# Half-slab loads, statistics in three pieces and later folds in the head of a spectral and feed-forward kernel

## The chip, the cores and the metric

The kernel runs on one core of one Trainium2 chip. The metric is the device time of one execution in microseconds (us). A run also gives the mean clock granted to TensorE. Medians are of all executions of a run; ratios, with their 95% intervals, use executions of the fast state only. "PE" is TensorE, "PEld" its weight load, "DVE" VectorE, "ACT" ScalarE, "POOL" GpSimd, "SP" SyncE.

## The reference, cut to what matters

```python
x = A_x                                # 1 x 2048 x 640, bf16
xn = _layernorm(x, axis=-1)
X = rfft2(xn); X = X * (w_r + 1j*w_i)  # w_r, w_i: 2048 x 321
s = irfft2(X)                          # spectral branch
g = _silu((_gelu(xn @ w_gate) * (xn @ w_up)) @ w_down)   # feed-forward branch, 640 -> 1536 -> 640
# ... the output is x + s * g
```

Both branches need the layer norm of x. TensorE does the feed-forward products and the Fourier transforms, which are products with tables.

## The kernel before

x is held as 16 slabs of 128 rows by 640. Each task of the kernel (a load, a pass, a group of products) is given to a planner written in the kernel itself, with a cost, a rank and what it must follow. The planner simulates the engines and fixes in which order each engine gets its instructions, and on which engine a copy runs. So a changed cost or dependency can change the order of instructions anywhere in the program.

```python
# loads of the first slabs
nc.scalar.dma_start(out=X[:, 1, :], in_=xv[:, 1, :])
nc.scalar.dma_start(out=X[:, 3, :], in_=xv[:, 3, :])
# ...
load_x(0, 1)                       # slab 0, whole, SyncE
x_in[1] = x_in[0]
load_x(2, 3)

# statistics of a slab on VectorE: one task
def moments(e):
    for g in range(2):
        nc.vector.bn_stats(out=STAT[:, n1, 6*g:6*g+6], in_=x[:, 320*g:320*g+320])
    nc.vector.bn_aggr(out=MVA[:, n1, :], in_=...)
    nc.vector.tensor_scalar_add(out=var, in0=var, scalar1=1e-5)
t = add(moments, "DVE", (1200, 1340), (2, n1), after=after, use=[sX])
# then root: (var)^-0.5 on GpSimd; apply: normalise on VectorE; turn_pe: transpose on TensorE and copy out
# ...
        if n1 % 2:                 # two slabs normalised: fold them for the spectral branch
            fold(n1 // 2, [aps[n1 - 1], aps[n1]])
```

`fold` is four adds and subtracts on VectorE, two pairs of products on TensorE ("fold products"), two copies and a store. Two more parts come up in the experiments. The spectral weights are gathered row by row, 32 times, by GpSimd:

```python
for pm in range(2):
    for ri, wsrc in enumerate((A_w_r, A_w_i)):
        nc.gpsimd.indirect_dma_start(out=sw.tile[:, pm, ri, 0:L], out_offset=None, in_=wsrc,
            in_offset=bass.IndirectOffsetOnAxis(ap=LANE[:, 2*G+pm:2*G+pm+1], axis=0))
```

and four tables (TI, I1T, IM, IT) are loaded from ScalarE's queue near 65 us.

## Time and profile before

| | before |
|---|---|
| three runs, first set | 218.63, 215.86, 215.78 us |
| the run that was profiled | 205.17 us, span 203.0, clock 1.0 |
| PE busy | 196.6 us, 97% of the span |

And in the list of transfers, the gathers have a time to landing, 3.0 us:

```profile
WF<-in_A_w_r_dram,LANE POOLq DMA_INDIRECT x16, 3.0
```

### The profile page before, as it was taken

What the parts mean: (1) busy time and instruction counts of PE and PEld (TensorE: products, weight loads), DVE (VectorE), ACT (ScalarE), POOL (GpSimd) and SP (SyncE); (2) the same over time, 40 slices, a digit from 0 to 9 for tenths busy, and PEclk for the clock granted to TensorE, in tenths of its full rate; (3) what the DMA queues carried; (4) which work ended last, traced back from release to release, by engine and by line L of the source; (5) the groups of instructions that cost most, each with busy time, mean ns of one, the idle gap of its engine ahead of it and who ended that gap; (6) DMA issues with size and microseconds to landing.
All of it is one profiled execution on the core that took longest, in us unless ns stands there. A gap on an engine that the chain in (4) does not pass through costs nothing.

```text
span 203.0 us, 3956 instructions
## 1 busy us (share of the span) xinstructions
PE 196.6 (97%) x1481; PEld 115.7 (57%) x1481; DVE 160.7 (79%) x340; ACT 108.4 (53%) x185; POOL 57.4 (28%) x83
## 2 busy tenths in 40 slices
PE   7899999999999999999999999999999999999991
PEld 2584444576545555577765544457764555556781
DVE  2899989998235289999999999932489799997764
ACT  2686963344524567788786633323454565454421
POOL 3514532065027505476478200000002022221100
PEclk9999999999999999999999999999999999999999
DMA  6999999799499601143143501119402244333422
GB/s 184 313 318 338 355 338 253 120 296 177 151 300 277 220 3 28 37 120 112 37 127 115 181 0 66 66 66 336 184 0 59 74 129 118 85 99 116 126 76 65
DMA packets 30947, 30.78 MB, mean 152 GB/s; under 512 B 10545, under 2 KB 27457, under 8 KB 30929
## 3 DMA queue, kind: packets, MB, share of 16 engines
q1 hardware_dynamic: 27696, 24.16, 39.7%
q0 software_dynamic: 2368, 5.30, 10.5%
q10 hardware_dynamic: 864, 1.09, 1.7%
q8 instruction: 11, 0.18, 0.4%
q14 instruction: 8, 0.06, 0.1%
HBM read 20.70 MB, written 7.86 MB: 141 GB/s over the span
## 4 chain that ended last, share of the span: by engine, by line
PE 78%; DMA 9%; DVE 5%; SPq 4%; ACT 1%; issue 1%; ACTq 0%; DVEq 0%
PE pg L808 19%; PE pu L808 19%; PE pu L868 12%; PE pg L868 12%; DMA X<-in_A_x_dram 5%; SPq L296 4%; DMA D<-mc 3%; PE sp L621 3%; PE sp L754 3%; PE sp L696 2%; PE sp L730 2%; PE sp L591 2%; DVE uT L824 1%; PE sp L614 1%; PE sp L748 1%
## 5 line engine op out<-in xcount | busy, mean ns | idle before, releaser
L808 PE MATMUL pg<-xnT,Wg 128*128 128x512 bf16 (+1 forms) x270 | 60.7, 355 | 0.0
L808 PE MATMUL pu<-xnT,Wu 128*128 128x512 bf16 (+1 forms) x270 | 60.7, 355 | 0.0
L820 ACT ACTIVATE ge<-pg 128x512 bf16<-128x512 f32 x48 | 28.6, 596 | 38.9 <-PE pg L808 38.5
L868 PEld LDWEIGHTS <-uT 128*128 128x128 bf16 x396 | 37.5, 98 | 13.2
L824 DVE TENSOR_TENSOR uT<-pu,ge 128x512 bf16<-128x512 f32 x48 | 33.0, 689 | 12.6 <-PE pu L808 11.3
L808 PEld LDWEIGHTS <-Wg 128*128 128x128 bf16 x270 | 24.6, 98 | 22.7
L808 PEld LDWEIGHTS <-Wu 128*128 128x128 bf16 x270 | 24.2, 98 | 20.8
L868 PE MATMUL pg<-Wd,uT 128*128 128x320 bf16 (+2 forms) x204 | 31.8, 293 | 0.0
L868 PE MATMUL pu<-Wd,uT 128*128 128x320 bf16 (+1 forms) x192 | 31.0, 297 | 0.0
L289 ACT CAST ma<-sp 128x644 bf16<-128x644 f32 (+1 forms) x29 | 23.1, 795 | 13.3 <-PE sp L754 6.6
L833 POOL DMA_DIRECT2D xr<-in_A_x_dram x16 | 8.6, 547 | 72.8 <-DVE res L856 72.8
L547 POOL DMA_INDIRECT WF<-in_A_w_r_dram,LANE x16 | 16.7, 1047 | 18.0 <-DVE mc L661 15.0
L547 POOL DMA_INDIRECT WF<-in_A_w_i_dram,LANE x16 | 17.4, 1085 | 4.9 <-issue 4.6
L415 POOL TENSOR_TENSOR RSTD<-MVA,mh 128x1 f32<-128x1 f32 x16 | 9.5, 595 | 22.6 <-DVE MVA L399 22.1
L877 ACT ACTIVATE th<-pg 128x320 f32<-128x320 f32 (+2 forms) x17 | 7.2, 426 | 16.1 <-PE pg L868 15.6
L882 DVE SCALAR_TENSOR_TENSOR G<-th,pg 128x320 bf16<-128x320 f32 (+2 forms) x17 | 8.0, 468 | 7.9 <-ACT th L877 7.9
L882 DVE SCALAR_TENSOR_TENSOR G<-th,pu 128x320 bf16<-128x320 f32 (+1 forms) x16 | 7.7, 479 | 4.1 <-ACT th L877 4.1
L397 DVE BATCH_NORM_STATS2 STAT<-X 128x6 f32<-128x320 bf16 x18 | 7.9, 481 | 3.1 <-DMA X<-in_A_x_dram 3.1
L289 ACT CAST IU<-sp 128x640 bf16<-128x640 f32 x13 | 9.0, 691 | 2.5 <-PE sp L696 2.3
L289 ACT CAST mc<-sp 128x640 bf16<-128x640 f32 x11 | 7.2, 693 | 3.4 <-PE sp L491 3.4
L877 ACT ACTIVATE th<-pu 128x320 f32<-128x320 f32 (+1 forms) x16 | 7.0, 438 | 3.1 <-PE pu L868 2.4
L674 DVE TENSOR_TENSOR R<-Y 64x644 bf16<-64x644 bf16 x16 | 7.9, 491 | 0.4
(79 smaller groups left out, 238.0 us busy)
## 6 DMA issues: line engine op xcount, KB each, us to landing
BU<-D SPq DMA_DIRECT2D x8, 640.0 KB, 7.1
D<-mc SPq DMA_DIRECT2D x8, 320.0 KB, 4.1
D<-IU SPq DMA_DIRECT2D x8, 320.0 KB, 2.4
xr<-in_A_x_dram POOLq DMA_DIRECT2D x16, 160.0 KB, 3.0
out_dram<-res SPq DMA_DIRECT2D x15, 160.0 KB, 1.8
Wg<-in_B_w_gate_dram SPq DMA_DIRECT2D x6, 320.0 KB, 6.1
Wu<-in_B_w_up_dram SPq DMA_DIRECT2D x6, 320.0 KB, 7.1
Wd<-in_B_w_down_dram SPq DMA_DIRECT2D x2, 960.0 KB, 8.5
```

Of the source, the lines that this page charges most:

```text
L289: return nc.scalar.copy(out=out, in_=in_) if e == "ACT" else nc.vector.tensor_copy(out=out, in_=in_)
L296: return add(lambda e: nc.sync.dma_start(out=out() if callable(out) else out, in_=in_() if callable(in_) else in_), "SP", (430, 430), rank ...
L397: nc.vector.bn_stats(out=STAT[:, n1, 6 * g:6 * g + 6], in_=x[:, 320 * g:320 * g + 320])
L415: nc.gpsimd.tensor_tensor(out=rstd, in0=var, in1=mh, op=ALU.pow)
L547: nc.gpsimd.indirect_dma_start(out=sw.tile[:, pm, ri, 0:L], out_offset=None, in_=wsrc, in_offset=bass.IndirectOffsetOnAxis(ap=LANE[:, 2 * ...
L808: nc.tensor.matmul(ps.tile[:, lo:hi], lhsT=w[:, c, t * P:(t + 1) * P], rhs=xnT[:, c, grp * 512 + lo:grp * 512 + hi], start=(c == 0), stop= ...
L820: nc.scalar.activation(out=ge.tile, in_=pg.tile, func=ACT.Gelu_apprx_tanh)
L824: nc.vector.tensor_tensor(out=u.tile, in0=pu.tile, in1=ge.tile, op=ALU.mult)
L833: nc.gpsimd.dma_start(out=sx.tile, in_=xv[:, n1, :])
L868: nc.tensor.matmul(ps.tile[:, 0:hi - lo], lhsT=uT[grp, t].tile[:, j * P:(j + 1) * P], rhs=Wd[:, t, lo:hi], start=(t == 0), stop=(t == 11))
L877: nc.scalar.activation(out=th.tile[:, 0:hi - lo], in_=ps.tile[:, 0:hi - lo], func=ACT.Tanh, scale=0.5)
L882: nc.vector.scalar_tensor_tensor(out=G2.tile[:, lo:hi], in0=th.tile[:, 0:hi - lo], scalar=1.0, in1=ps.tile[:, 0:hi - lo], op0=ALU.add, op1 ...
```

## The change

The intent is an earlier first product. What runs before the first 512-wide product, some 14 us, is called the head. The halves of slabs 0 and 1 go to both queues, so that slab 0 is there first. The statistics are three tasks, so that the normalise of slab 0 can go ahead of slab 1's last piece. And the first folds wait until slab 3 is normalised.

```diff
-    nc.scalar.dma_start(out=X[:, 1, :], in_=xv[:, 1, :])
+    for n in range(2):
+        nc.scalar.dma_start(out=X[64:P, n, :], in_=xv[64:P, n, :])
@@
-    load_x(0, 1)
-    x_in[1] = x_in[0]
+    for n in range(2):
+        seq[0] += 1
+        x_in[n] = dma(X[0:64, n, :], xv[0:64, n, :], (0, -4, seq[0]), 163840, use=[sX])
     load_x(2, 3)
-    t = keep_warm(4, [t, x_in[0]], 0)
-    keep_warm(3, [t, x_in[1]], 1)
+    t = keep_warm(3, [t, x_in[0]], 0)
+    keep_warm(2, [t, x_in[1]], 1)
@@
-            t = add(moments, "DVE", (1200, 1340), (2, n1), after=after, use=[sX])
+            t = add(lambda e: half(e, 0), "DVE", (445, 445), (2, n1), after=after, use=[sX])
+            t = add(lambda e: half(e, 1), "DVE", (445, 445), (2, n1), after=[t], use=[sX])
+            t = add(moments, "DVE", (345, 450), (2, n1, -1), after=[t])
@@
-        if n1 % 2:
+        if n1 == 3:
+            for j in range(2):
+                fold(j, [aps[k] for k in range(4)])
+        elif n1 % 2 and n1 > 3:
             fold(n1 // 2, [aps[n1 - 1], aps[n1]])
# ... and planner constants: start of the DMA wire 2600 -> 1900, hold of the normalises
# 700 (slabs 0, 1) -> 250 (slabs 0 to 3), later statistics behind slab 3's copy, a few costs
```

More of the change, by code (lines that the diff above doesn't have):

```diff
@@ L25 @@
 DUMP = None
+VERB = False
 def make_tables():
@@ L135, in __init__ @@
         self.tasks, self.slots = [], {t: [] for t in bufs}
-        self.wire = 2600.0
+        self.wire = 1900.0
     def add(self, emit, eng, cost, rank, after=(), new=(), use=(), size=0, slow=1.0, hold=0):
@@ L194, in run @@
             self.free[e] = now + occ
+            if VERB: print(f"{now:9.0f} {occ:6.0f} {t.done or 0:9.0f} {e} {t.emit.__qualname__.split('kernel.<locals>.')[-1]} {t.rank}")
             t.done = now + lat
@@ L358, in go @@
                                  start=True, stop=True, skip_group_check=True)
-        return add(go, "PE", (n * 430, n * 430), (0, -9), after=after, new=[] if heat.users else [heat], use=[idle, sX] + ([heat] if heat.users else []))
+        return add(go, "PE", (n * 390, n * 390), (0, -9), after=after, new=[] if heat.users else [heat], use=[idle, sX] + ([heat] if heat.users else []))
     t = add(blank, "DVE", (330, 400), (0, -9), new=[idle])
     t = keep_warm(6, [t])
-    load_x(0, 1)
-    x_in[1] = x_in[0]
+    for n in range(2):
+        seq[0] += 1
+        x_in[n] = dma(X[0:64, n, :], xv[0:64, n, :], (0, -4, seq[0]), 163840, use=[sX])
     load_x(2, 3)
-    t = keep_warm(4, [t, x_in[0]], 0)
-    keep_warm(3, [t, x_in[1]], 1)
+    t = keep_warm(3, [t, x_in[0]], 0)
+    keep_warm(2, [t, x_in[1]], 1)
     x_in[3] = tab_in["id"] = x_in[2]
@@ L392, in stats, with half @@
         eng = engs[0]
-        after = [x_in[n1]] + ([aps[3]] if n1 > 3 else [])
+        after = [x_in[n1]] + ([turned[3]] if n1 > 3 else [])
+        def half(e, g):
+            nc.vector.bn_stats(out=STAT[:, n1, 6 * g:6 * g + 6], in_=x[:, 320 * g:320 * g + 320])
         def moments(e):
-            for g in range(2):
-                nc.vector.bn_stats(out=STAT[:, n1, 6 * g:6 * g + 6], in_=x[:, 320 * g:320 * g + 320])
             nc.vector.bn_aggr(out=MVA[:, n1, :], in_=STAT[:, n1, :].rearrange("p (g s) -> p g s", g=2))
@@ L427, in go @@
                                     op0=ALU.subtract if eng == "DVE" else ALU.add, op1=ALU.mult)
-        return add(go, "DVE", (360, 510), (1, n1, 0), hold=700 if n1 < 2 else 0, after=[root], new=[sxn] if new else [], use=[sX] if new else [sX, sxn])
+        return add(go, "DVE", (430, 530), (1, n1, 0), hold=250 if n1 < 4 else 0, after=[root], new=[sxn] if new else [], use=[sX] if new else [sX, sxn])
     def turn_pe(n1, ap):
```

## The prediction

> **What bounds the kernel now.** I read the page's busy shares first, then busy time in stretches, then the head in order of time.
>
> ```profile
> PE 196.6 (97%) x1481; PEld 115.7 (57%) x1481; DVE 160.7 (79%) x340; ACT 108.4 (53%) x185; POOL 57.4 (28%) x83
> ...
> PE   7899999999999999999999999999999999999991
> DVE  2899989998235289999999999932489799997764
> ```
>
> TensorE (PE) is busy 97% of a span of 203.0 us. A busy PE need not be an efficient one, so I checked start times: in the steady stretch five 512-wide matmuls start every 1.08 us, 0.216 us each, with nothing between groups. PE is therefore the bound by order of work. The question is only where it idles or does useless work. By stretch (columns: stretch, length, then busy us and instruction counts of PE, weight load, VectorE (DVE), ScalarE (ACT), GpSimd (POOL), then clock, DMA share, GB/s):
>
> ```profile
> 7.00:8.00 1.00, 0.45 (x5) 0.28 (x5) 0.55 (x3) 0.34 (x1) 0.83 (x3) 1.00 1.09 349
> 8.00:9.00 1.00, 0.93 (x16) 0.93 (x17) 0.97 (x4) 0.80 (x2) 0.44 (x1) 1.00 1.20 306
> 9.00:10.00 1.00, 0.98 (x19) 0.81 (x17) 0.96 (x5) 0.25 (x1) 0.68 (x1) 1.00 1.20 307
> ...
> 35.00:40.00 5.00, 4.87 (x29) 2.48 (x27) 5.00 (x12) 1.57 (x4) 0.00 (x0) 1.00 0.74 119
> ...
> 195.00:203.00 8.00, 3.96 (x41) 3.36 (x39) 4.16 (x13) 1.81 (x5) 0.00 (x0) 1.00 0.18 61
> ```
>
> From 10 us to the last matmul near 199 us PE loses about 0.13 us in all. After that come 4 us of tail (last tanh, gate, residual, store), which the change does not touch. What is left is the head: the first useful product (gate weights by slab 0) starts at 8.40 us. Before it PE runs 13 throwaway matmuls[...], and the transposes of slabs 0 and 1. The head in order of time (start, length, engine, line, operation, then idle before it and what ended it):
>
> ```profile
> 0.73 0.39 ACTq L340 DMA_DIRECT2D X<-in_A_x_dram  x1
> 0.73 0.89 SPq L296 DMA_DIRECT2D X<-in_A_x_dram  x2
> 4.22 0.89 DVE L397 BATCH_NORM_STATS2 STAT<-X 128x6 f32<-128x320 bf16 x2 [3.06 <-DMA X<-in_A_x_dram]
> 5.45 0.88 DVE L397 BATCH_NORM_STATS2 STAT<-X 128x6 f32<-128x320 bf16 x2
> 5.62 0.57 POOL L415 TENSOR_TENSOR RSTD<-MVA,mh 128x1 f32<-128x1 f32 x1 [3.06 <-DVE MVA L399]
> 6.61 0.15 DVE L399 TENSOR_SCALAR MVA<-MVA 128x1 f32<-128x1 f32 x1
> 6.68 0.44 DVE L425 TENSOR_SCALAR s<-X,MVA,RSTD 128x640 bf16<-128x640 bf16 x1
> 7.17 0.45 PE L436 MATMUL sp<-ident,s 128*128 128x128 bf16 x5 [0.27 <-DVE s L425]
> 7.66 0.69 ACT L289 COPY xnT<-sp 128x640 bf16<-128x640 bf16 x1 [0.80 <-PE sp L436]
> 8.40 0.44 PE L808 MATMUL pg<-xnT,Wg 128*128 128x128 bf16 x5
> ```
>
> The reader is to see one chain: slab 0 arrives, statistics, power of -1/2 on GpSimd, normalise, transpose, copy, first product. Two links are longer than need be. The data are visible at 4.22 us. And 1/std of slab 0 is ready at 5.62 + 0.57 = 6.19, but the normalise starts at 6.68, because slab 1's whole statistics stand before it on VectorE: 0.49 us lost.
>
> [...] slabs 0 and 1 start together at 0.73, and the DMA share is 1.05 in the 3 to 4 us stretch. So the halves do not move bytes faster; they change which bytes come first. [...] the throwaway matmuls start 0.41 to 0.43 us apart until 6.31 us, and at the transposes at 7.17 us the weight loads stand 0.056 us apart.
>
> **The change, part by part.**
>
> 1. *Halves over both queues.* In the DMA view of the first 9 us in 40 slices of 0.225 us, I summed GB/s by slice: 164 KB had been moved by about 2.8 us, 328 KB by about 3.35. Before, slabs 0 and 1 interleave, so slab 0's last byte comes near 3.35 and is seen at 4.22. After, both halves of slab 0 go first, so it needs 164 KB: about 0.5 us earlier. I take its statistics to start at 3.7. Slab 1 should be seen near 4.2 as before. Slabs 2 and 3 stand behind the same bytes; one more issue on each queue (0.43 us) is hidden as the DMA engines are full by then. Seen by ACT at 5.08 before; I allow up to 5.2.
>
> 2. *Statistics in three pieces.* No work is added: two halves of 0.44 us, then aggregate and add (0.40 us to the end). It lets the normalise of slab 0 slip between. By hand, with the durations above: slab 0 halves 3.7 to 4.6, its aggregate and add end at 5.0, POOL 5.1 to 5.7, slab 1 halves 4.95 to 5.8, normalise of slab 0 at 5.8 (before 6.68: 0.9 earlier). Slab 1's aggregate then waits for it, ends at 6.6, its power 6.65 to 7.25, its normalise at about 7.35 (before 7.56).
>
> 3. *Transpose and copy of slab 0.* Transposes at about 6.3, ready for the copy at 6.8. ACT holds slab 2's two passes, which ended at 6.86 before and will not end earlier. So copy 6.88 to 7.57, first product at about 7.65, against 8.40: 0.75 us earlier. Here ACT takes over a little of the wait.
>
> 4. *PE from there to the first 512-wide product.* Before, 8.40 to 14.38 = 5.98 us: 16 groups of 0.28 (4.48), transposes of slabs 2 and 3 (0.56), one fold product (0.54), so 0.40 of bubbles. After: 16 groups, three transposes (0.84), the fold product later instead: 5.32 us, from 7.65 to 12.97. Before without the fold: 13.84. So PE is ahead by 0.87 us, if no bubble comes.
>
> 5. *Folds after the norm of slab 3.* Eight VectorE operations of 0.40 us (3.2 us) move behind the normalises. Two of them stood between slab 2's normalise at 9.20 and slab 3's at 10.37, so slab 3 comes about 1 us earlier: by hand its normalise is at about 8.9, its columns are ready near 10.3, and PE wants them at about 11.7. The later folds do not hurt: spectral products start near 63 us, and PE has feed-forward work until then.
>
> 6. *Two throwaway matmuls fewer, new cost constants.* Off the path. The constants alter the order that the kernel's own planner chooses all through the program. I cannot price that; PE's list is the same work.
>
> Sum: 0.87 us, all in the head, passing to the end because PE is dense behind it. 215.86 - 0.87 = 214.99.
>
> **Rivals.**
>
> *A: the arrival does not move.* If the four halves interleave on the engines, or first-byte ramp dominates (GB/s climbs from 28 to 273 between 1.6 and 2.9 us), slab 0 is still seen at 4.2. Only the split helps: normalise at 6.3, gain some 0.35 us, 215.5.
>
> *B: another wait takes its place.* The up weights: about 1,360 KB precede their end, which the summed stretches put near 6.6 us, seen perhaps at 7.4, against a need at 7.9. ACT's slab 2 passes: if slab 2 arrives 0.3 later, the copy moves with it. [...] Each would leave 0.2 to 0.6 of gain: 215.3 to 215.7.
>
> *C: the moved folds or the new order open holes later.* VectorE is at 95% or more from 80 to 130 us, and PE lives there on feed-forward work put between. Against it: PE was at 10.00 of 10.00 in each of those stretches, so there is stock. If the new order is unlucky, 0.5 to 1.5 us come back and the time is 215.5 to 216.5.
>
> *D: hidden.* That an earlier head is absorbed wholly (215.9) would need PE idle time later; the stretches show nearly none.
>
> **Range and chances.** I weigh the main line at about 60%, A and B at 25%, C at 15%. Before's three times span 215.78 to 218.63, so one slow run can lift a median. Predicted 215.0 us, range 214.1 to 216.3. Faster by over 2% needs 4.3 us, more than half of all time before the first useful product: 1%. Slower by over 2% needs a broken plan or a slow median: 2%. Within 2%: 97%.
>
> **What would show it.** Slab 0's first statistics at 3.7, not 4.2; its normalise between slab 1's halves and aggregate, at 5.8; first product near 7.65; the first 512-wide product near 13.0; no PE hole over 0.3 us between 8 and 13 us; last matmul near 198. Wrong: slab 0 not earlier, the copy of slab 0 waiting on ACT past 7.0[...], or PE under 4.8 of 5 in any later stretch.

## More of the kernel before

By its time, the profile that I read for the prediction is one of the quick kind of chip (which chip it was is not on record), and the times are of the slow kind.

Beside what the prediction shows, two views of this profile will matter. First the timeline near 65 us (start, length, engine, line, operation; in brackets the idle time before it and what ended it):

```profile
64.90 1.24 PE L808 MATMUL pg<-xnT,Wg 128*128 128x512 bf16 x5
...
65.38 0.44 ACTq L321 DMA_DIRECT2D IT<-tab_it  x1
66.18 0.60 ACT L820 ACTIVATE ge<-pg 128x512 bf16<-128x512 f32 x1 [1.15 <-PE pg L808]
```

The gate product that starts at 64.90 ends at 66.14, and the gelu that reads it starts at 66.18, 0.04 us later. Then the busy times by stretch (columns: stretch, length, busy us and instruction count of PE, PEld, DVE, ACT, POOL, then clock, DMA share, GB/s):

```profile
62.00:76.00 14.00, 14.00 (x111) 7.52 (x109) 7.99 (x13) 7.54 (x10) 5.88 (x7) 1.00 0.50 153
90.00:125.00 35.00, 35.00 (x284) 21.36 (x283) 33.73 (x65) 23.76 (x37) 15.74 (x16) 1.00 0.32 95
```

TensorE has no idle time in either stretch.

## The result, and the profile after

| | before | after |
|---|---|---|
| median of 6 runs, same set | 216.41 us (215.78 to 218.63) | 213.46 us (211.47 to 214.04) |
| ratio of fast runs | | 0.9866 (0.9817 to 0.9915) |
| profiled run | span 203.0, quick kind | span 209.7, clock 0.991, slow kind |

A ratio is the mean time of one kernel's fast runs over the mean of the other's of the same rounds, so it is not quite the ratio of the medians. The change gained 2.9 us where at most 1.8 lay in the range: the direction was right, the size was not, and the gain is under 2%. The page after, and its stretches:

```profile
PE 196.4 (94%) x1463; PEld 117.1 (56%) x1479; DVE 158.5 (76%) x337; ACT 109.9 (52%) x188; POOL 55.6 (27%) x83
...
PE   7599999999999789997998999999999999999991
```

```profile
7.00:8.00 1.00, 0.45 (x5) 0.38 (x6) 0.96 (x5) 1.00 (x3) 0.58 (x2) 0.98 1.04 325
8.00:9.00 1.00, 0.56 (x6) 0.56 (x6) 0.83 (x5) 0.39 (x1) 0.92 (x3) 0.50 1.09 337
9.00:10.00 1.00, 1.00 (x13) 1.00 (x11) 0.92 (x3) 0.30 (x1) 0.33 (x1) 0.50 1.20 301
...
35.00:40.00 5.00, 4.95 (x27) 2.49 (x27) 4.50 (x12) 2.48 (x4) 0.73 (x1) 1.00 0.90 118
...
62.00:76.00 14.00, 12.07 (x84) 6.28 (x84) 5.20 (x7) 4.63 (x7) 6.71 (x8) 1.00 0.54 175
90.00:125.00 35.00, 32.52 (x278) 20.83 (x279) 31.08 (x60) 21.86 (x33) 18.84 (x19) 1.00 0.34 100
```

Three things stand out. PE's work is the same, 196.4 us busy, but the span is 6.7 us longer than in the profile before. The head is not faster: from 8 to 10 us the clock column says 0.50, and only 6 and 13 products start where 16 and 19 did before. And PE is idle for 1.93 us between 62 and 76 and for 2.48 us between 90 and 125, where it was idle for nothing before. The head in order of time:

```profile
3.73 0.89 DVE L400 BATCH_NORM_STATS2 STAT<-X 128x6 f32<-128x320 bf16 x2 [2.58 <-DMA X<-in_A_x_dram]
5.71 0.89 DVE L400 BATCH_NORM_STATS2 STAT<-X 128x6 f32<-128x320 bf16 x2 [0.66 <-DMA X<-in_A_x_dram]
6.03 0.74 ACT L407 ACTIVATE th<-X 128x640 bf16<-128x640 bf16 x1 [1.66 <-DMA X<-in_A_x_dram]
6.52 0.43 DVE L432 TENSOR_SCALAR s<-X,MVA,RSTD 128x640 bf16<-128x640 bf16 x1
7.00 0.45 PE L443 MATMUL sp<-ident,s 128*128 128x128 bf16 x5 [0.68 <-DVE s L432]
8.44 0.69 PE L818 MATMUL pg<-xnT,Wg 128*128 128x128 bf16 x5 [0.98 <-ACT xnT L291]
```

Slab 0 comes earlier, at 3.73, and slabs 1 and 2 come later, at 5.71 and 6.03; they were there by 5.45 and 5.08. The first product is at 8.44, so the head alone explains no gain at all in this execution. The stretch near 66 us and the transfers:

```profile
65.78 1.24 PE L818 MATMUL pg<-xnT,Wg 128*128 128x512 bf16 x5
...
67.60 0.44 ACTq L323 DMA_DIRECT2D IT<-tab_it  x1
70.54 0.60 ACT L830 ACTIVATE ge<-pg 128x512 bf16<-128x512 f32 x1 [3.27 <-PE sp L584]
```

```profile
WF<-in_A_w_r_dram,LANE POOLq DMA_INDIRECT x16
```

The gate product of 65.78 ends at 67.02, and its gelu starts at 70.54, 3.5 us later. ScalarE had nothing else to do but issue table loads until 68.04. And the gathers have no time to landing any more, but neither has any other transfer on this page (the loads of BU had 7.1 us before), so this tells of signals that are missing from the record and not of slower gathers. The late gelu belongs to the kind of chip and not to the change, as is shown next.

### The profile page after: what moved, and what is told of

Read it like the earlier page. It is cut to its first block, busy times and chain, and to the rows that moved or that the text cites.

```text
span 209.7 us, 3946 instructions
## 1 busy us (share of the span) xinstructions
PE 196.4 (94%) x1463; PEld 117.1 (56%) x1479; DVE 158.5 (76%) x337; ACT 109.9 (52%) x188; POOL 55.6 (27%) x83
## 4 chain that ended last, share of the span: by engine, by line
PE 88%; DVE 4%; DMA 2%; ACT 2%; issue 2%; SPq 1%; DVEq 0%
PE pu L818 24%; PE pg L818 23%; PE pg L878 12%; PE pu L878 12%; PE sp L706 3%; PE sp L631 3%; PE sp L764 3%; PE sp L740 2%; DMA X<-in_A_x_dram 2%; PE sp L601 2%; PE sp L497 2%; PE sp L624 1%; PE sp L758 1%; DVE uT L834 1%; PE sp L443 1%
## 5 line engine op out<-in xcount | busy, mean ns | idle before, releaser
L818 PE MATMUL pg<-xnT,Wg 128*128 128x512 bf16 (+1 forms) x262 | 60.0, 358 | 1.3 <-ACT xnT L291 1.0
L818 PEld LDWEIGHTS <-Wu 128*128 128x128 bf16 x270 | 24.8, 99 | 21.6 <-issue 0.4
L422 POOL TENSOR_TENSOR RSTD<-MVA,mh 128x1 f32<-128x1 f32 x16 | 10.3, 646 | 19.6 <-DVE MVA L404 19.0
L291 ACT CAST IU<-sp 128x640 bf16<-128x640 f32 x12 | 8.1, 692 | 2.5 <-PE sp L706 2.5
L291 ACT CAST Z<-sp 128x1024 bf16<-128x1024 f32 x7 | 7.0, 1017 | 4.3 <-PE sp L706 1.9
L291 ACT CAST mc<-sp 128x640 bf16<-128x640 f32 x13 | 8.4, 698 | 0.8 <-PE sp L498 0.8
```

What stands on the lines that cost most here:

```text
L291: return nc.scalar.copy(out=out, in_=in_) if e == "ACT" else nc.vector.tensor_copy(out=out, in_=in_)
L422: nc.gpsimd.tensor_tensor(out=rstd, in0=var, in1=mh, op=ALU.pow)
L818: nc.tensor.matmul(ps.tile[:, lo:hi], lhsT=w[:, c, t * P:(t + 1) * P], rhs=xnT[:, c, grp * 512 + lo:grp * 512 + hi], start=(c == 0), stop= ...
```

## The experiments

**Set 1, a slow chip (before 213.62 us, 211.51 to 215.03, 11 runs): what comes from the loads, and what from the order?** The kernel before and the changed one again, and the two halves of the change crossed. `e3` is the kernel before with half loads and no other difference, `e4` the changed kernel with whole loads; the order is the same as in the kernel each comes from.

```diff
# e3: old order, half loads
-    load_x(0, 1)                                   (and slab 1 whole from ScalarE)
+    X[0:64, 0], X[0:64, 1] from SyncE; X[64:128, 0], X[64:128, 1] from ScalarE, in the old task's place
# e4: changed order, whole loads
-    halves
+    slab 0 whole from SyncE, slab 1 whole from ScalarE, in the new tasks' places
```

> The kernel before, unchanged, for its profile on a chip where it takes its usual time: the profile shown of it (span 203.0 us, 205.17 us) is 10.7 us shorter than its timed runs (median 216.41 us). Theory H (only the head changed): the usual run has the same dense TensorE from the first product on and a later first product[...]. Theory O (order): the usual run has TensorE holes of 5 to 10 us in all between 60 and 130 us, in the spectral stage, as the profile of the changed kernel has (about 6 us there); then the profile shown of before was of a lucky execution. [...] Expected time 216 us, ratio 1.00.

> The changed kernel again, for a second profile and its ratio on this chip. The first profile has its first product at 8.44 us, half clock from 8.0 to 11.4 us and about 6 us of TensorE holes between 60 and 120 us. Theory H: ratio 0.985 to 0.99 again. Theory G: if the half-clock window comes and goes by execution, times spread by about 1.7 us. Theory O: holes at the same places as in the first profile.

> The kernel before with the loads of slabs 0 and 1 as partition halves over both queues, and nothing else: the order of instructions on TensorE, VectorE, ScalarE and GpSimd is exactly that of before. If the loads bring the gain, the ratio to before is near 0.987; if they bring only slab 0's earlier arrival (0.5 us), 0.997 to 0.998; if the late arrival of slab 1 (seen at 5.7 us in the profile of the changed kernel, against 4.2 or earlier in that of before) costs as much, 1.00 or above.

> The changed kernel with the loads of before (slab 0 whole on one queue, slab 1 whole on the other), and nothing else: the order of instructions on TensorE, VectorE, ScalarE and GpSimd is exactly that of the changed kernel. If the gain is in the order (theory O, or the pieces of the statistics and the folds), the ratio to before stays at 0.985 to 0.99, or is lower as slab 1 comes earlier; if the halves bring it, the ratio goes to 1.00.

| run | median us | ratio to before (95%) |
|---|---|---|
| e1, before again | 213.31 | 1.0014 (0.9970 to 1.0058) |
| e2, after again | 211.77 | 0.9905 (0.9859 to 0.9951) |
| e3, old order, half loads | 213.25 | 0.9988 (0.9942 to 1.0035) |
| e4, new order, whole loads | 211.37 | 0.9900 (0.9851 to 0.9948) |

Within about 0.5% the half loads bring nothing; the gain is in the order. And e1 is the first look at the kernel before on a slow chip. (Its profiled execution, 211.76 us at a clock of 0.996, is one of the faster ones; 8 of the 11 of this set have 0.983 to 0.992.)

```profile
65.50 1.24 PE L808 MATMUL pg<-xnT,Wg 128*128 128x512 bf16 x5
...
66.27 0.44 ACTq L321 DMA_DIRECT2D IT<-tab_it  x1
70.58 0.60 ACT L820 ACTIVATE ge<-pg 128x512 bf16<-128x512 f32 x1 [4.65 <-PE pu L808]
```

```profile
62.00:76.00 14.00, 11.21 (x83) 5.95 (x81) 4.67 (x6) 5.42 (x8) 6.83 (x8) 1.00 0.57 182
90.00:125.00 35.00, 32.98 (x285) 21.23 (x283) 30.98 (x61) 24.21 (x36) 18.21 (x19) 1.00 0.33 100
```

The same product and the same gelu as in the profile before, but 3.84 us between the product's end and the gelu (70.58 less 65.50 less 1.24) instead of 0.04. TensorE is idle for 2.79 us in the first stretch and 2.02 us in the second. So the late gelu is no work of the change; it belongs to the kernel before on this chip. The engines themselves are not slower there: the instructions of VectorE take 161.0 us in e1 and 160.7 in the quick profile, those of ScalarE 108.0 and 108.4.

To see where time is gained I read how far TensorE lags behind its own work: the start of a product, less the time that all columns before it take at full pace. The lag grows where PE waits, and also where it does not: by 3.4 us from 65 to 186 us of work in the quick profile, where PE is busy for 188.83 of the 189 us from 10 to 199. So the rows are read against each other. In us, at so much work done:

```
work done                      5.5     15     40     60     65    100    186
old order, quick (shown)      8.26   8.34   8.73   8.80   9.24  10.87  12.62
old order, slow  (e1)         7.72   7.80   8.48   9.40  12.70  17.50  19.26
new order, slow  (e4)         7.09   7.16   8.14   8.21  10.90  15.69  17.46
```

Of the 1.80 us between e1 and e4 at the end, 0.63 stand after the head. Part of that is lost by 40 us of work (0.34), and by 60 it is 1.19: fold products no longer wait for copies between 38 and 51 us (PE is busy for 18.19 of the 19 us from 35 to 54 in e1, for all 19.00 in e4). By 65 it is 1.80, since the hole near 73 us is shorter (idle from 62 to 76: 2.79 us in e1, 2.34 in e4), and behind that nothing is added.

**Set 2, which landed on a quick chip (before 204.87 us, 204.58 to 205.92, 11 runs): spliced orders, and the table loads moved.** For a splice the planner is bypassed: its order and engines are written out as a list, the first part from one kernel and the rest from the other. The kernel with the whole list of one kernel gives that kernel back, instruction for instruction (but for throwaway products). The loads are whole, and both splices have the 11 throwaway products of the changed kernel, not the 13 of the old one.

```diff
-        for t in plan.run():
-            t.emit(t.on)
+        for w in ORDER.split():            # e5: new order's tasks of its first 14 us, then the old order
+            t = plan.tasks[int(w[:-1])]     # e6: old order's tasks of its first 14.6 us, then the new order
+            t.on = ENG[w[-1]]
+            t.emit(t.on)
# e7 (new order, whole loads) and e8 (before): the four tables
-   nc.scalar.dma_start(out=flat(tiles[k]), in_=tabs[k])
+   nc.sync.dma_start(out=flat(tiles[k]), in_=tabs[k])
```

> Whole loads. Every instruction that the changed plan starts in its first 14 us stands in the changed order (split statistics, folds after the norm of slab 3, two throwaway products fewer); everything behind it stands in the order and on the engines of the kernel before, written out as a fixed list. Theory H (the gain is the head's, passed on whole): all of the gain of the changed order with whole loads, that is about 2 us under the kernel before (ratio 0.990). Theory M (the head gives only what the lag of TensorE showed at 5.5 us, 0.6 us, and the rest comes from the order behind it, where the products of the folds no longer wait for the copies between 38 and 51 us and the hole near 70 us is shorter): 0.4 to 0.8 us under the kernel before, ratio 0.997, with holes at 38 to 51 us still there.

> Whole loads. The first 14.6 us of the plan in the order of the kernel before (statistics in one go, first fold before slab 3's norm), everything behind it in the order and on the engines of the changed kernel, as a fixed list. Theory H: nothing, ratio 1.00. Theory M: 1.2 to 1.6 us under the kernel before, ratio 0.993, and no holes over 0.3 us at 38 to 51 us. If both this run and the one with the new head gain, and the two gains add up to about 2 us, the parts are independent.

> Changed order with whole loads, and one more thing: the four table loads that ScalarE issues near 65 us are issued by SyncE at the same place of the program. Theory T (ScalarE stands still for 2.5 to 4 us behind its own table loads, and that makes the hole near 70 us): the gelu behind them starts at once, the hole of TensorE at 72 to 73 us goes, and the time falls by 1.5 to 2.5 us against the same order with the loads on ScalarE, to a ratio of about 0.98 against the kernel before. Theory S (ScalarE waits for something else, and the loads only stand beside it): the same gap is there at the same place and the ratio stays 0.990.

> The kernel before, with the four table loads of ScalarE issued by SyncE at the same place. Theory T: the hole of about 3 us near 73 us goes, the ratio is 0.985 to 0.99. Theory S: no change, ratio 1.00. If the change gained because its order made this stall shorter, the two kernels with the loads on SyncE differ by less than the two with them on ScalarE (under 2 us).

| run | median us | ratio to before (95%) |
|---|---|---|
| e5, new head, old rest | 205.24 | 1.0002 (0.9978 to 1.0026) |
| e6, old head, new rest | 207.43 | 1.0115 (1.0088 to 1.0142) |
| e7, new order, tables on SyncE | 206.04 | 1.0064 (1.0034 to 1.0095) |
| e8, before, tables on SyncE | 204.88 | 0.9998 (0.9974 to 1.0021) |

The expectations were written for a before of 213, and none of the gains came. Here nothing of the change gains. e5's head is 0.65 us ahead after 5.5 us of work (lag 7.61 against 8.26), and it is lost at one fold product of the old order, which came too soon for VectorE:

```profile
24.83 0.39 PE L537 MATMUL sp<-mb,F1T 128*128 128x512 bf16 x1 [0.65 <-DVE mb L524]
```

e7 keeps its head's lead up to 95 us of work (lag 10.02 at 97, against 10.70 in the profile before), and then waits: by the lag 0.28 us near 103.7 and 0.91 us here, of which the view shows 0.74 as idle:

```profile
109.48 0.32 PE L624 MATMUL sp<-FT,zt 32*128 32x161 bf16 x7 [0.74 <-DVE IU L291]
```

That is a wait of the new order's own: a spectral product stands ahead of a copy that VectorE has not reached. The same hole, with 0.74 to 0.87 us idle, is in every profile with the new order behind the head, on both kinds of chip. e6 loses more than e7. In the three of its runs with a clock of 0.992, the profiled one among them, the head is one cause: the clock was at half from 8.1 to 11.5 us, and the first 512-wide product came 1.2 us later after slab 0 than in e8. The other three took 207.1 us on average, still 2.2 over the kernel before; what the seam of the splice costs was not separated.

**Set 3, a slow chip again (before 214.63 us, 211.91 to 217.40, 11 runs): is the stall ScalarE's own?**

```diff
# e12, kernel before, right behind the last table load on ScalarE
+                if k == "it":
+                    for _ in range(3):
+                        nc.scalar.copy(out=still, in_=flat(T2)[:, 0:1024])
```

> The changed kernel as it is, a third time, because the calls so far landed on two kinds of chip: the kernel before took 213.6 us in the first call of experiments and 204.9 us in the second. Theory K (what the change is worth depends on the kind of chip: on the slow kind, where ScalarE stands still behind its table loads, the new order hides part of that; on the quick kind there is nothing to hide and the new order's own waits near 104 and 109 us cost what its head saves): if this call's before is near 205 us, ratio 1.00 to 1.01, not faster; if it is near 213.5 us, ratio 0.985 to 0.992 again. Theory O (the new order is better anywhere): ratio 0.99 on either.

> The kernel before with the four table loads of ScalarE issued by SyncE, again, for the other kind of chip. If before is near 213.5 us here: theory T (the stall belongs to ScalarE's own loads) says 208 to 211 us, the 3 us hole near 73 us gone and perhaps what follows from it; theory S (ScalarE waits for something else) says 213.5. If before is near 205: 204.9 as in the call before.

> The changed order with whole loads and the tables on SyncE, again, for the other kind of chip. If before is near 213.5 us here: theory T says 208 to 209.5 us, and no longer better than the kernel before with the same edit if the change's gain was only in hiding the stall; theory S says 211.4. If before is near 205: 206.0 as in the call before.

> The kernel before with three copies of 128x1024 (about 3 us) put on ScalarE right behind its last table load, which do nothing for the result: the stall of the slow kind of chip made on purpose. On a chip where before takes 205 us: if that stall alone is what parts the two kinds, 210 to 213 us, with a hole of TensorE of about 3 us near 73 us and further holes between 90 and 115 us; if it is only one of several causes, 207 to 209 us. On a chip where before takes 213.5: 214 to 217 us if the copies add to the stall, 213.5 if they run inside it.

| run | median us | ratio to before (95%) |
|---|---|---|
| e9, after | 212.17 | 0.9931 (0.9867 to 0.9996) |
| e10, before, tables on SyncE | 213.78 | 1.0002 (0.9944 to 1.0060) |
| e11, new order, whole loads, tables on SyncE | 210.05 | 0.9842 (0.9778 to 0.9906), unclear at 2% |
| e12, before, 3 us of copies | 214.84 | 1.0054 (0.9984 to 1.0124) |

The theory that ScalarE stands still behind its own loads has fallen: without them (e10) the kernel before takes the same time, and e11's gelu still waits 3.25 us. (e11 is 2.1 us under e9, but differs from it by the whole loads as well as by the tables, so I draw nothing from that.) e12 shows the same from the other side. Three copies of 3.2 us fitted into the wait and cost little or nothing:

```profile
66.28 3.20 ACT L326 COPY still<-T 128x1024 bf16<-128x1024 bf16 x3 [0.82 <-issue]
70.13 0.60 ACT L826 ACTIVATE ge<-pg 128x512 bf16<-128x512 f32 x1 [0.64 <-PE pu L814]
```

The gelu came at 70.13 with the copies and at 70.58 without (in e1, on another slow chip). So ScalarE is waiting for something other than itself, and I read it as a signal that arrives late. I listed the recorded signals of TensorE (its semaphore counter) in that stretch, in us:

```
before, quick: 63.10 63.55 64.00 65.08 66.16 67.23 67.46 67.68 68.76 69.84 70.48 71.56
before, slow (e1): 63.70 64.15 64.89 67.72 70.56 72.01 72.06 72.12 72.19 72.26 73.94
```

On the quick chip there is one per group of products. On the slow one they come 2.8 us apart, and then several at once. Such gaps stand on slow chips at 64.9 to 72, 90 to 93, 99 to 101 and 107 to 113 us in e1, each time while packets of GpSimd's gathers run (which also run from 83 to 88 us without a gap). The trace of e1 keeps fewer signals (113 of all from 58 to 76 us, against 298), but what is missing is of the DMAs (81 against 249): of this counter of TensorE it has 224 records in all, against 227 in the quick profile. So the bursts are not gaps left by lost records. Whether the signal came late, or only its record, the list cannot tell; the late gelu is a measured start.

**Set 4, a slow chip (before 216.25 us, 213.74 to 217.56, 27 runs): the splices again, and the gathers taken away.** e15 and e16: plain loads of as many rows of the same size, on GpSimd at the same places. Their outputs are wrong, which doesn't matter for the times. e16 is the changed kernel as it is, with its half loads.

```diff
-    nc.gpsimd.indirect_dma_start(out=sw.tile[:, pm, ri, 0:L], out_offset=None, in_=wsrc,
-        in_offset=bass.IndirectOffsetOnAxis(ap=LANE[:, 2*G+pm:2*G+pm+1], axis=0))
+    nc.gpsimd.dma_start(out=sw.tile[:, pm, ri, 0:L], in_=wsrc[P*(2*G+pm):P*(2*G+pm)+P, :])
```

> The changed order for the first 14 us and the old order behind it, whole loads, again, for the slow kind of chip. Theory M (head 0.6 us, the rest of the gain from the order behind it): ratio 0.996 to 0.998. Theory H (all of it from the head): 0.990. If this call's before is near 205 us: 1.000 as in the earlier call, since the head's gain was lost again at 24.8 us to a product of the first fold.

> The old order for the first 14.6 us and the changed order behind it, again, for the slow kind of chip. Theory M: 0.993 to 0.996. Theory H: 1.00. On the quick kind it was 1.0115, so a ratio under 1.00 here would show that the changed order behind the head is worth something only on the slow kind.

> Wrong result on purpose: the kernel before with its 32 indirect gathers of spectral weights replaced by plain loads of as many rows of the same size, issued by GpSimd at the same places. Theory Q (on the slow kind of chip semaphore updates are held up while the indirect gathers run): if before is near 213.5 us here, this falls to 203 to 207 us, and the 3 us hole near 73 us and the bursts of TensorE's semaphore updates go. Rival (the slow kind is slower for another reason): over 211 us. If before is near 205 us: 203 to 205.

> Wrong result on purpose: the changed kernel as it is, halves included, with the same plain loads in place of the gathers. Theory Q: with nothing to hide, the change is worth what the quick kind of chip showed: 204 to 207 us, not faster than the kernel before with plain loads, and possibly 1 us slower, from its own waits near 104 and 109 us. Theory O (the new order is better anywhere): 2 us under the kernel before with plain loads.

| run | median us | ratio to before (95%) |
|---|---|---|
| e13, new head, old rest | 215.96 | 0.9978 (0.9949 to 1.0007) |
| e14, old head, new rest | 212.88 | 0.9882 (0.9826 to 0.9937) |
| e15, before, plain loads (wrong) | 205.13 | 0.9519 (0.9476 to 0.9563) |
| e16, after, plain loads (wrong) | 208.01 | 0.9633 (0.9579 to 0.9686) |

These four settle where the gain is. On a slow chip the head is worth 0.2%, some 0.5 us and not clear of noise, and the order behind it 1.2%, some 2.6 us. The same order behind the head costs 1.15% on a quick chip (e6). What it gains on the slow chip of this set is idle time of TensorE, most of it in the spectral stretch, e13 first and e14 below:

```profile
90.00:125.00 35.00, 30.41 (x272) 20.34 (x274) 28.82 (x57) 23.84 (x36) 18.66 (x19) 1.00 0.32 93
```

```profile
90.00:125.00 35.00, 32.53 (x279) 20.96 (x280) 31.20 (x60) 22.45 (x33) 18.86 (x19) 1.00 0.34 100
```

Idle time of 4.59 and 2.47 us: 2.1 of the 4.4 us between the spans of these two executions (the fast runs differ by 2.7 us on average). On the chip of set 1 this stretch gained nothing (idle 2.02 us in e1, 2.29 in e4), so where the order gains differs, and by what waits it gains is not shown. Without gathers the kernel before takes on a slow chip what it takes on a quick one, 205.13 against 204.87 us, and its gelu near 66 us follows its product (65.29 and 1.24) at once again:

```profile
65.29 1.24 PE L806 MATMUL pg<-xnT,Wg 128*128 128x512 bf16 x5
66.57 0.60 ACT L818 ACTIVATE ge<-pg 128x512 bf16<-128x512 f32 x1 [1.15 <-PE pg L806]
```

And the changed kernel is then the slower of the two by 2.9 us, more than I had expected. Part of that is its head: four of e16's six runs had a clock of 0.980 to 0.992 and took 207.97 to 208.75 us; the two with a clock of 1.0 took 206.5, which is 1.3 us over e15's median.

**Set 5, the chip of set 4 (before 216.31 us, 214.55 to 217.38, 11 runs): a correct kernel with fewer gathers.** The unmirrored rows (pm = 0) of groups 1 to 7 lie 128 rows apart in blocks of four, so a plain strided load can fetch them. The mirrored rows run backwards and stay gathers. So 14 of 32 gathers go, in the old order (e17) and in the changed order with whole loads (e18).

```diff
+    if G == 0 or pm:
         nc.gpsimd.indirect_dma_start(...)          # as before
+        continue
+    for h in range(2):
+        r0 = 8 * G + 4 * h
+        nc.gpsimd.dma_start(out=sw.tile[64*h:64*h+64, pm, ri, 0:L],
+                            in_=wsrc.rearrange("(k r) f -> k r f", r=P)[:, r0:r0 + 4, :])
```

> Correct result: the kernel before, where 14 of the 32 indirect gathers (the unmirrored rows of groups 1 to 7, which lie at an even stride) are 28 plain strided loads of 64 rows each, on GpSimd at the same places; 18 gathers stay. Theory Q: on the slow kind of chip, where all 32 replaced took the time from 216 to 205 us, about half of that, 208 to 212 us; on the quick kind within 1 us of the kernel before. Rival (the first few gathers near 65 us do all the harm): less, over 213 us.

> Correct result: the changed order with whole loads and the same 14 gathers replaced. Theory Q: the hold is shorter, so the changed order has less to hide: 207 to 210 us on the slow kind, and its advantage over the kernel before with the same edit falls from 2 to 2.5 us to 0 to 1.5 us. On the quick kind 1 us slower than the kernel before. Theory O: it stays 2 us or more ahead of the kernel before with the same edit.

| run | median us | ratio to before (95%) |
|---|---|---|
| e17, before, 18 gathers left | 205.57 (205.48 to 206.38) | 0.9521 (0.9480 to 0.9561) |
| e18, new order, 18 gathers left | 205.88 (205.43 to 207.51) | 0.9536 (0.9490 to 0.9583) |

Both results are correct. The gain is 10.7 us, far more than the half that I expected, and the advantage of the changed order is gone. e17's stretches:

```profile
62.00:76.00 14.00, 13.89 (x106) 7.44 (x107) 7.82 (x13) 7.37 (x10) 6.25 (x9) 1.00 0.55 164
90.00:125.00 35.00, 34.64 (x277) 21.19 (x278) 33.37 (x63) 23.23 (x35) 15.50 (x22) 1.00 0.33 96
```

The idle time is 0.11 and 0.36 us, against 2.79 and 2.02 in e1, and the gelus between 60 and 78 us start 0.04 to 0.09 us after their products.

A part of the gain is clock. In the four slow sets of experiments 48 of 60 executions of the kernel before have a clock under 0.993, on the quick chip none of 11, and none of the 12 of e15 and e17. In set 5 the two executions of the kernel before at 0.997 or more took 214.7 us on average, the other nine 216.5. The profiles of e12 and e13 show where it goes: a hole of TensorE near 70 us, and behind it half clock for 3.4 us. In e13 (the column behind POOL's is the clock):

```profile
70.40:73.80 3.40, 1.32 (x6) 0.38 (x4) 0.67 (x2) 0.89 (x2) 0.95 (x1) 1.00 0.42 129
73.80:77.30 3.50, 2.83 (x17) 1.39 (x18) 1.12 (x2) 2.00 (x3) 0.00 (x0) 0.51 0.00 0
```

So in these two executions the hole cost twice, once as a wait and once as clock. Not every hole did: in e1 TensorE is idle for 2.79 us before 73.22 us, and the clock is 1.00 from 70 to 80.

e17 beats both the kernel before and the changed one on a slow chip; on a quick chip it was not run.

What stays open: which property of the slow chips makes the engines wait (late signals are the reading that fits, not a measurement), and why 14 gathers fewer are enough. Plain loads from GpSimd do not do it (e15). GpSimd's own work is not the cause: it is busy for 56.4 us in e1 and 56.6 in e17. Nor are its packets slower: from 60 to 125 us they take 109 ns on average in e1 and 120 in the quick profile. Gaps in TensorE's list of signals are still there in e17, up to 3.1 us, but TensorE no longer starves. And the changed kernel itself was not run on a quick chip: e6, e7 and e16 are what speaks for it being the slower one there.

## Why the prediction was wrong, step by step

**The bound.** TensorE is the bound, as said, but "From 10 us to the last matmul near 199 us PE loses about 0.13 us in all" held for that one execution only. In e1, on a slow chip, TensorE was idle for 4.8 us in two stretches. The prediction took its start from the timed runs, 215.86, and its mechanism from a profiled run of 205.17. The profile could not show what lay between them. Of the 6.6 us between its span and that of e1, 4.9 are idle time of TensorE and 1.7 longer busy time; how the whole 10.7 us divide was not profiled, and clock is in them too.

**The failed step** is the sum: "0.87 us, all in the head, passing to the end because PE is dense behind it", and with it step 6, where the order of the planner was set aside with "I cannot price that; PE's list is the same work". The order was the larger part: 2.6 us on a slow chip (e14), against 0.5, not clear of noise, for the head (e13). Rival C named the order as a risk, as a loss of 0.5 to 1.5 us; on a quick chip it is about that or more (by the medians 1.2 us in e7, 2.6 in e6). The other sign was not considered, because where TensorE never waits an order can only lose.

**Step 1, halves.** The runs say: slab 0 is seen at 3.66 on average in five profiles with halves (3.47 to 3.73) and at 3.99 in fifteen with whole loads (3.60 to 4.36). So it gains 0.33, not 0.5, and 4.22 was one draw from a spread. The allowance for the others failed: ScalarE's pass over slab 2 starts at 6.09 on average with halves (5.48 to 7.01; 7.01 is e2, whose profile is of the slow state, and without it the mean is 5.86) and at 4.77 with whole loads, 1.1 to 1.3 us later where 0.1 was allowed. In the profile after, "one more issue on each queue (0.43 us)" was not what it cost: ScalarE's two half issues took 1.23 us, against 0.39 for one whole slab, so slab 3's issue slid to 1.99 us. On SyncE, which loads slab 2, three issues took until 2.57 us, where two took until 1.62, so slab 2's own issue ended 0.95 us later. Rival B's "if slab 2 arrives 0.3 later, the copy moves with it" came true with about four times that delay, and I take that for the reason why the halves bring nothing.

**Steps 2 and 3, split and copy.** Right in mechanism. Counted from slab 0's arrival, the first product comes 4.18 to 4.23 us later in the old order with whole loads (nine profiles) and 3.75 us later in the new one (e4, e5, e7, e11, e13, e18 alike). That is 0.45 us; rival A had put the split alone at 0.35. With halves it is 4.61 to 4.72 us in the new order (5.74 in e2, slow state), since the copy of slab 0 waits behind ScalarE's pass over slab 2: at 7.71 in the profile after, past the 7.0 that the prediction gave as a sign of being wrong.

**Step 4, to the first 512-wide product.** Predicted 0.87 us ahead of the old order without the fold. Counted from slab 0's arrival again: 10.16 to 10.17 us in the old order (profile before, e1, e8, e12), 9.6 in e4, e5, e11 and e18. So 0.57 with whole loads, where nothing else intervenes: e17 takes 10.19 and e10 and e15 10.6 in the old order, e7 9.73 and e13 10.19 in the new. In the profile after it is 11.94: of the 2.3 us more than in e4, 0.96 lie before the first product, from the late slab 2, and 1.4 behind it, at half clock. The sum of step 4 also took the 0.40 us of bubbles to vanish ("if no bubble comes"), for which it gave no reason.

**Half clock in the head.** In the profile after the clock is at half from 7.96 to 11.38 us. In the 3.4 us before, TensorE had been busy for 1.5 us, with idle times of 0.77, 0.68 and 0.5 us. In e3, e4 and e16 the runs with a clock of 0.992 or less are 1.5 to 1.8 us longer on average than those at 0.997 or more (in e9 and e14 by 0.5 at most), and all six runs of the changed kernel in the first set had 0.989 to 0.991. Step 6 called the two throwaway products that were taken out "off the path". They may not be: half clock stands in the head of six profiles (after, e2, e6, e9, e14, e16; e2 is of the slow state), all with 11 throwaway products and a first product 4.19 us or more after slab 0; the six with 11 and a first product at 3.75 have none, and neither have the eight with 13. No run put the two back, so this is not shown.

**Step 5, folds.** Right: no fold product delays the head, and the fold products of the later pairs no longer wait for copies, which is the 0.55 us between 15 and 60 us of work in set 1.

## What to carry to other kernels

Before you predict from a profile, hold its own time against the timed runs; if they differ by more than the effect you look for, the profile shows another machine than the one that is timed. A gain that comes with a new order of instructions is to be tested as an order, by splicing the two orders, and on more than one chip: here the same order behind the head was 1.2% faster on one kind and 1.2% slower on the other. And row gathers by indirect DMA deserve a try with plain strided loads wherever the rows allow it, even for less than half of them: on a slow chip that was worth 4.8%, more than three times the change. On a quick one it was not run.

## What the traces showed of the hardware

- In the profiles of three sets of runs ScalarE started late behind the products that it waited for, in stretches where GpSimd's indirect gathers run; in the quick set, with the same gathers, it did not. A gelu started 3.84 us after the end of its product in e1, 3.5 us in the profile after, 0.04 us in the quick profile, and in e11 ScalarE stood idle for 3.25 us before it; the kernel took 216.3 us against 204.9, and 205.6 with 14 of 32 gathers replaced.
- TensorE stood idle for 4.8 us in two stretches in e1, with all of the gathers, and for 0.5 in e17, with 18.
- The regular part of the gathers could be taken out first: it was 14 of 32, its plain loads were still issued by GpSimd, and it was worth 10.7 us on a slow chip.
- To issue two loads of 64 partitions took 1.23 us on ScalarE in the profile after, and one of 128 partitions 0.39 in the profile before. (The whole slab behind the two halves took 0.85, against 0.45 in its old place, so the partitions alone may not be the cause.)
- In the profiles of fast executions here the clock fell to half seven times before the tail. In the 3.4 us before, TensorE was busy for 1.46 us in the profile after and for 1.32 in e13. That alone does not decide it: in the 3.4 us up to 73.22 in e1, with 2.79 of them idle, it was busy for some 0.6, and the clock stayed at 1.00.
